# Seven block products in place of eight for gate and value in the second expert layer

## The chip, the core and the metric

The program runs on one core of one Trainium2 chip. The metric is the device time of one execution in microseconds (us). Its engines are TensorE (PE in the profile, with PEld for its weight loads), VectorE (DVE), ScalarE (ACT), GpSimd (POOL) and SyncE (SP), which issues every DMA.

## What is computed

Causal attention with a cumulative bias, then two gated expert layers, the first after a normalisation. With 2304 tokens, model width 512 and hidden width 1536 per layer, this is the part that the change touches:

```python
def _moe2_ref(x, w_gate, w_val, w_out):
    g = x @ w_gate                          # 2304x512 @ 512x1536
    silu = g * (1.0 / (1.0 + np.exp(-g)))
    val = x @ w_val                         # 2304x512 @ 512x1536
    return (silu * val @ w_out)             # 2304x1536 @ 1536x512
```

## The kernel before, in words

Every operand of a matmul is split into a high and a low part (`H`, `L`, type fp32r), and a product is three matmuls: H·H, L·H and H·L. Tokens lie in the columns: `TGROUPS` are four groups of 512 tokens and one of 256. The hidden width is cut into 12 blocks of 128 (`KF`, index `f`), the model width into 4 (`KD`).

The program has three stretches. The first holds attention and the gate and value products of the first layer. The second is the output product of the first layer: per group and `f`, the hidden block `hh` is loaded from DRAM, split on ACT (`hH`, L1050) and DVE (`hL`, L1052), and multiplied into four PSUM banks by 12 matmuls (`out_mm`, L1061); at a group's end ACT evicts the four banks (`out_store`, L1070) and the result goes to DRAM as `x1_d`. The third is the second layer: `load_x1` (L1089 to L1093) loads and splits a group of `x1`; per `f`, `gate_value` (L905) does 24 matmuls into two banks of the ring `mo`, `hidden` (L912, L914, L917) applies the gate on ACT and DVE, `split_h` splits it, and `out_mm` multiplies the block before into four other banks.

Weights come as 64-bit floats. `convert` loads a piece (L405, 512 KB) into a staging buffer (`raw` or `cvs`) and makes floats of it on ACT (`cvy`, L408) and DVE (L410), then `H` on ACT (L415) and `L` on DVE or POOL (L419). The second layer's gate and value weights (`load_gv`, 24 pieces) and output weights (`load_o`, 12 pieces) are converted during the second stretch, the last pieces through the one buffer `cvs`, and stay in SBUF.

The order of the work on each engine is fixed when the program is built: `Plan.run` gives each operation a cost and a priority (`pri`, the lower the earlier) and puts it on its engine's queue. On the chip each engine works through its queue in order and waits at each instruction for what it needs. `SLACK = 1500.0` in `Plan` keeps a matmul that another engine released back by up to 1500 ns as long as other matmuls are ready.

Of the kernel before, what the change touches and what calls it, by code (L numbers as in the profile page):

```python
# [22 lines left out]
P = 128  # L23
# [18 lines left out]
class Buf:  # L42
# [9 lines left out]
    def __call__(self):  # L52
        if self.tile is None:
            self.tile = self.make() if self.share is None else self.make(self.place)
        return self.tile

# [222 lines left out]
def tile_kernel(  # L279
# [729 lines left out]
    cvs_o = buf("o", "cvs", [P, 2 * DM], I32)  # L1009
    cvy_o = buf("o", "cvy", [P, 512], F32)  # L1010

    def load_o(src, f, pri):
        H, L = (buf("o", f"o{z}{f}", [P, DM], F32R) for z in "HL")
        if f == 0:
            plan.ops[-1]
        convert(src[f * P:(f + 1) * P, :], (H, L), 0, cvs_o, cvy_o, pri)
        return H, L

    for k in [cvs_o, cvy_o] + [buf("o", f"o{z}{f}", [1], F32) for z in "HL"
                                      for f in range(KF)] + \  # L1020
            [buf("o", f"h{z}{i}", [1], F32) for z in "hHL" for i in range(2)]:
        plan.live[k.key] = list(plan.live["o"])
    clear([cvy_o], -900)
    W1o = [load_o(w_o, f, P_ATT + 1000 + f) for f in range(KF)]
# [10 lines left out]
    def m2buf(tag, shape, dtype, name=None):  # L1035
        b = buf("m2", tag, shape, dtype, name)
        if b.key not in plan.live:
            plan.live[b.key] = list(plan.live["m2"])
        return b

    P2 = 1.0e5

    def hring(z, dtype):
        return ring("o", f"h{z}", 2, [P, 512], dtype)

    def split_h(hh, n, pri):
        H, L = hring("H", F32R), hring("L", F32R)
        op(ACT, c_act(n) + 35, lambda en: en.activation(H()[:, :n], hh()[:, :n], ACTF.Copy),  # L1050
           r=[hh], w=[H], pri=pri)
        op(DVE, c_tt(n), lambda en: en.tensor_tensor(  # L1052
            out=L()[:, :n], in0=hh()[:, :n], in1=f32(H()[:, :n]), op=ALU.subtract),
           r=[hh, H], w=[L], pri=pri, port=True)
        return H, L

    def out_mm(acc_, Wo, HL, f, n, pri):
        for d in range(KD):
            c = slice(d * P, (d + 1) * P)
            for i, (w, x) in enumerate(((0, 0), (0, 1), (1, 0))):  # L1060
                op(PE, c_mm(n), lambda en, d=d, c=c, w=w, x=x, i=i: en.matmul(  # L1061
                    acc_[d]()[:, :n], Wo[w]()[:, c], HL[x]()[:, :n], start=(f == 0 and i == 0),
                    stop=(f == KF - 1 and i == 2)), r=[(Wo[w], 0), HL[x]],
                   w=[acc_[d]] if f or d or i else [*acc_, "claim"], pri=pri)

    def out_store(acc_, n, dst, key, pri, places=("oo0", "oo1") * 2, any_engine=False):
# [111 lines left out]
```

## Time and profile before

| | before |
|---|---|
| median of 3 runs | 1134.37 us (1133.91 to 1135.48) |
| span of the profiled execution | 1134.0 us |
| PE busy | 1113.0 us (98%) |
| PEld busy | 1002.2 us (88%) |
| DVE busy | 583.3 us (51%) |
| ACT busy | 512.4 us (45%) |
| POOL busy | 181.2 us (16%) |
| DMA moved | 112.51 MB, mean 99 GB/s |

The page gives one execution, with its span as its own time; it lies 0.37 us under the median and inside the range of the runs. A matmul's duration in the records is longer than its share of the time, since matmuls overlap: the step from one start to the next is the price of one.

### The profile page before, as it was taken

What the parts mean: (1) busy time and instruction counts of PE and PEld (TensorE: products, weight loads), DVE (VectorE), ACT (ScalarE), POOL (GpSimd) and SP (SyncE); (2) the same over time, 40 slices, a digit from 0 to 9 for tenths busy, and PEclk for the clock granted to TensorE, in tenths of its full rate; (3) what the DMA queues carried; (4) which work ended last, traced back from release to release, by engine and by line L of the source; (5) the groups of instructions that cost most, each with busy time, mean ns of one, the idle gap of its engine ahead of it and who ended that gap; (6) DMA issues with size and microseconds to landing.
All of it is one profiled execution on the core that took longest, in us unless ns stands there. A gap on an engine that the chain in (4) does not pass through costs nothing.

```text
span 1134.0 us, 18700 instructions
## 1 busy us (share of the span) xinstructions
PE 1113.0 (98%) x6724; PEld 1002.2 (88%) x6724; DVE 583.3 (51%) x1606; ACT 512.4 (45%) x1135; POOL 181.2 (16%) x276
## 2 busy tenths in 40 slices
PE   8799999999999999999989999999999999999998
PEld 5599999999999999999878888888888888888898
DVE  7797778787787666547733234432222222222222
ACT  5877767667666753436744334323111211211121
POOL 3344434323333200100011000001000100100000
PEclk9999999999999999999999999999999999999999
DMA  5984443423323204359665443202000100100010
GB/s 162 291 254 117 123 133 116 124 83 110 107 85 95 62 29 147 115 160 309 203 216 175 149 126 120 89 19 75 1 1 1 65 1 1 47 1 1 1 38 19
DMA packets 70092, 112.51 MB, mean 99 GB/s; under 512 B 11568, under 2 KB 39216, under 8 KB 70000
## 3 DMA queue, kind: packets, MB, share of 16 engines
q1 hardware_dynamic: 70000, 111.33, 31.9%
q8 instruction: 53, 0.87, 0.3%
q14 instruction: 39, 0.32, 0.1%
HBM read 87.61 MB, written 23.67 MB: 98 GB/s over the span
## 4 chain that ended last, share of the span: by engine, by line
PE 48%; DMA 3%; DVE 2%; ACT 1%; issue 1%; SPq 0%; DVEq 0%; ACTq 0%
PE mo L905 26%; PE sps L1061 9%; PE tp L1061 9%; PE mo L1061 5%; DMA cvs<-in_w_gv 1%; DMA raw<-in_w_gv 1%; DMA h_d<-hh 1%; ACT H L415 1%; DVE raw L410 1%; DVE hL L1052 0%; ACT cvy L408 0%; DVE L L419 0%; DMA hh<-h_d 0%; DVE hh L917 0%; SPq L937 0%
## 5 line engine op out<-in xcount | busy, mean ns | idle before, releaser
L905 PE MATMUL mo<-xL,H 128*128 128x320 f32 (+1 forms) x768 | 228.0, 297 | 0.0
L905 PE MATMUL mo<-xH,H 128*128 128x320 f32 (+1 forms) x768 | 227.8, 297 | 0.0
L905 PE MATMUL mo<-xH,L 128*128 128x320 f32 (+1 forms) x768 | 227.7, 297 | 0.0
L914 DVE SCALAR_TENSOR_TENSOR t<-t,mo 128x256 f32<-128x256 f32 (+2 forms) x156 | 81.1, 520 | 218.3 <-ACT t L912 217.3
L905 PE MATMUL mo<-x1H,H 128*128 128x512 f32 (+1 forms) x480 | 176.6, 368 | 0.0
L905 PE MATMUL mo<-x1H,L 128*128 128x512 f32 (+1 forms) x480 | 176.6, 368 | 0.0
L905 PE MATMUL mo<-x1L,H 128*128 128x512 f32 (+1 forms) x480 | 176.6, 368 | 0.0
L912 ACT ACTIVATE t<-mo 128x256 f32<-128x256 f32 (+2 forms) x156 | 71.8, 460 | 209.5 <-PE mo L905 209.2
L1050 ACT ACTIVATE hH<-hh 128x512 fp32r<-128x512 f32 (+1 forms) x120 | 70.3, 587 | 179.8 <-DVE hh L917 126.0
L905 PEld LDWEIGHTS mo<-xH,H 128*128 128x128 f32 x768 | 144.2, 188 | 0.9 <-issue 0.2
L905 PEld LDWEIGHTS mo<-xL,H 128*128 128x128 f32 x768 | 144.3, 188 | 0.7 <-issue 0.2
L905 PEld LDWEIGHTS mo<-xH,L 128*128 128x128 f32 x768 | 144.2, 188 | 0.4
L1052 DVE TENSOR_TENSOR hL<-hh,hH 128x512 fp32r<-128x512 f32 (+1 forms) x120 | 79.6, 665 | 106.5 <-ACT hH L1050 106.1
L649 ACT ACTIVATE sc<-sc,col 128x512 f32<-128x512 f32 (+4 forms) x160 | 96.0, 600 | 65.0 <-DVE col L638 64.5
L917 DVE TENSOR_TENSOR hh<-t,mo 128x256 f32<-128x256 f32 (+2 forms) x156 | 81.1, 520 | 84.8 <-PE mo L905 81.2
L905 PEld LDWEIGHTS mo<-x1H,H 128*128 128x128 f32 x480 | 90.5, 189 | 15.0
L905 PEld LDWEIGHTS mo<-x1H,L 128*128 128x128 f32 x480 | 90.5, 189 | 14.8
L905 PEld LDWEIGHTS mo<-x1L,H 128*128 128x128 f32 x480 | 90.5, 189 | 14.8
L1093 POOL TENSOR_TENSOR x1L<-x1l,x1H 128x512 fp32r<-128x512 f32 (+1 forms) x20 | 24.4, 1226 | 417.6 <-ACT x1H L1091 392.2
L1061 PE MATMUL tp<-hH,oH 128*128 128x512 f32 (+1 forms) x192 | 69.8, 363 | 0.0
L1061 PE MATMUL tp<-hL,oH 128*128 128x512 f32 (+1 forms) x192 | 69.8, 364 | 0.0
L1061 PE MATMUL tp<-hH,oL 128*128 128x512 f32 (+1 forms) x192 | 69.6, 363 | 0.0
(133 smaller groups left out, 2017.0 us busy)
## 6 DMA issues: line engine op xcount, KB each, us to landing
raw<-in_w_gv SPq DMA_DIRECT2D x40, 511.8 KB, 6.0
hh<-h_d SPq DMA_DIRECT2D x48, 256.0 KB, 2.7
cvs<-in_w_o SPq DMA_DIRECT2D x24, 511.8 KB, 3.7
lq<-in_qk SPq DMA_DIRECT2D x32, 288.0 KB, 3.5
cb<-cum_d SPq DMA_DIRECT2D x32, 288.0 KB, 3.6
h_d<-hh SPq DMA_DIRECT2D x72, 128.0 KB, 2.5
vl<-in_vp SPq DMA_DIRECT2D x32, 160.0 KB, 2.3
x_d<-oo SPq DMA_DIRECT2D x16, 256.0 KB, 3.4
```

The source lines that it names most:

```text
L410: op(DVE, c_tt(n), lambda en: en.scalar_tensor_tensor(out=whole(U32), in0=whole(U32), scalar=13, in1=y().bitcast(U32), op0=ALU.logical_shi ...
L415: ACT: lambda en: en.activation(H()[:, cut], whole(), ACTF.Copy),
L649: op(ACT, c_act(o + m, 2) + 35, lambda en: en.activation(sc()[:m, :o + m], sc()[:m, :o + m], ACTF.Exp, scale=-1.0, bias=col()[:m, 0, t:t + 1],
L905: op(PE, c_mm(n), lambda en, a=a, x=x, c=c, k=k, i=i: en.matmul(ps()[:, :n], a()[:, c], x()[:, k, :n], start=(k == 0 and i == 0), stop=(k ...
L912: op(ACT, c_act(n), lambda en: en.activation(t()[:, :n], gp()[:, :n], ACTF.Tanh, scale=0.5), r=[gp], w=[t], pri=pri)
L914: op(DVE, c_tt(n), lambda en: en.scalar_tensor_tensor(out=t()[:, :n], in0=t()[:, :n], scalar=1.0, in1=gp()[:, :n], op0=ALU.add, op1=ALU.mu ...
L917: op(DVE, c_tt(n), lambda en: en.tensor_tensor(out=hh()[:, :n], in0=t()[:, :n], in1=vp_()[:, :n], op=ALU.mult), r=[vp_, t], w=[hh], pri=pri)
L1050: op(ACT, c_act(n) + 35, lambda en: en.activation(H()[:, :n], hh()[:, :n], ACTF.Copy), r=[hh], w=[H], pri=pri)
L1052: op(DVE, c_tt(n), lambda en: en.tensor_tensor(out=L()[:, :n], in0=hh()[:, :n], in1=f32(H()[:, :n]), op=ALU.subtract), r=[hh, H], w=[L], p ...
L1061: op(PE, c_mm(n), lambda en, d=d, c=c, w=w, x=x, i=i: en.matmul(acc_[d]()[:, :n], Wo[w]()[:, c], HL[x]()[:, :n], start=(f == 0 and i == 0) ...
L1093: op(POOL, c_ptt(n), lambda en, k=k, x=x: en.tensor_tensor(out=L()[:, k, :n], in0=x()[:, :n], in1=f32(H()[:, k, :n]), op=ALU.subtract), r= ...
```

## The change

The weights of gate and value for one `f` are seen as a 2x2 block matrix (gate and value in the rows, the two halves of the model width in the columns), and two token groups of 512 as the columns of the other factor. Strassen's scheme in Winograd's form gives the four result blocks with seven block products in place of eight. A block product is 6 matmuls of 128x512, so a pair of groups takes 42 matmuls per `f` in place of 48. Groups 0 and 1, and 2 and 3, are the pairs; group 4 (256 columns) is done as before, by `plain_unit`.

The four sums of weight blocks (`S1` to `S4`) are made per `f` in `load_w2`, and the four sums of token blocks (`T1` to `T4`) once per pair in `prepare_pair`. The loops are turned: `f` is outside, and per `f` come the first pair, group 4 and the second pair. The weights are therefore loaded and converted per `f`, through two staging buffers (`raws`, named `cvs0` and `cvs1`), into one of two places. A unit (`pair_unit`) uses three banks: bank `b` takes four products one upon the other and is copied out between them by ACT (`keep`); `c` takes two. Further sums are made on DVE (`add`) and POOL or DVE. The gated hidden blocks go to DRAM (`h2_d`), and the output product is a last stretch of its own (`out_layer`, also used for the first layer), whose weights are loaded and converted late in the last `f` and beside its first group. The output of the first layer stays in SBUF: `x1_d` and its loads are gone.

```diff
...
+    raws = [obuf(f"cvs{i}", [P, 2 * DM], I32) for i in range(2)]
...
+    def load_o(src, f, HL, pri):
+
+        H, L = HL
+        stage = raws[f % 2]
+        sub = [(POOL, c_ptt(DM)), (DVE, c_tt(DM))]
+        value = load_raw(src[f * P:(f + 1) * P, :], stage, pri)
+        op(ACT, c_act(DM) + 35, lambda en: en.activation(H(), value(), ACTF.Copy),
+           r=[stage], w=[H], pri=pri)
+        op(sub, 0, lambda en: en.tensor_tensor(out=L(), in0=value(), in1=f32(H()),
+                                               op=ALU.subtract),
+           r=[stage, H], w=[L], pri=pri, port=True)
...
+    def load_w2(f, pri):
+
+        H, L = (wide_buf(w2_tags[f % 2][z], [P, 2048], F32R, f"w2{'HL'[z]}") for z in range(2))
+        gate, val = (load_raw(w2_gv[f, :, 512 * z:512 * z + 512], raws[z], pri)
+                     for z in range(2))
...
+        for i, (a, b, sign, r) in enumerate((
+                (v1, v2, ALU.add, raws[1:]), (lambda: S(0), g1, ALU.subtract, [(sums, 0), raws[0]]),
+                (g1, v1, ALU.subtract, raws), (g2, lambda: S(1), ALU.subtract, [(sums, 1), raws[0]]))):
+            op(two, 0, lambda en, i=i, a=a, b=b, sign=sign: en.tensor_tensor(
...
+        for i, (src, r) in enumerate((
+                (gate, raws[:1]), (val, raws[1:]),
+                (lambda: sums()[:, :512], [(sums, 0), (sums, 1)]),
+                (lambda: sums()[:, 512:], [(sums, 2), (sums, 3)]))):
+            cut = slice(512 * i, 512 * i + 512)
+            op(ACT, c_act(512) + 35, lambda en, src=src, cut=cut: en.activation(
+                H()[:, cut], src(), ACTF.Copy), r=r, w=[(H, i)], pri=pri)
+            op([(POOL, c_ptt(512)), (DVE, c_tt(512))], 0, lambda en, src=src, cut=cut:
+               en.tensor_tensor(out=L()[:, cut], in0=src(), in1=f32(H()[:, cut]),
+                                op=ALU.subtract), r=[*r, (H, i)], w=[(L, i)], pri=pri, port=True)
...
+    def pair_unit(f, W, X, groups, pri):
+
+        u = units[0] % 2
+        units[0] += 1
+        b, c, d = [mo_bank() for _ in range(3)] if u == 0 else \
+            [bank(t) for t in ("sps0", "sps1", "tp0")]
+        p1, p5, u2, u3, t1, t2 = (spare_buf(6 * u + i) for i in range(6))
...
+        def product(ps, a, x, first, claims=()):
+            q = A_ROWS[a]
+            at = pri + step[0]
+            step[0] += 1
+            for kk in range(2):
+                cut = slice(q * 256 + kk * P, q * 256 + kk * P + P)
+                for i, (w, z) in enumerate(((0, "H"), (0, "L"), (1, "H"))):
+                    xx = X[x, z][kk]
+                    op(PE, c_mm(n), lambda en, w=w, xx=xx, cut=cut, kk=kk, i=i: en.matmul(
+                        ps()[:, :n], W[w]()[:, cut], xx(), start=first and kk == 0 and i == 0,
+                        stop=kk == 1 and i == 2, skip_group_check=not first), r=[(W[w], q // 2), xx],
+                       w=[ps] if kk or i else [ps, *claims], pri=at)
+
...
+        product(b, "A11", "B11", True, [c, d] if u == 0 else [])
+        keep(p1, b)
+        product(c, "S1", "T1", True)
+        keep(p5, c)
+        product(b, "S2", "T2", False)
+        keep(u2, b)
+        product(c, "S4", "B22", False)
+        add(u2, c)
+        product(b, "S3", "T3", False)
+        keep(u3, b)
+        product(d, "A12", "B21", True)
+        add(p1, d)
+        op([(POOL, c_ptt(n)), (DVE, c_tt(n))], 0, lambda en: en.tensor_tensor(
+            out=u3(), in0=u3(), in1=p5(), op=ALU.add), r=[u3, p5], w=[u3], pri=-1.0e4, port=True)
+        gated(u2, t2, u3, u3, groups[1])
+        product(b, "A22", "T4", False)
+        gated(p1, t1, b, lambda: b()[:, :n], groups[0])
...
-        a = banks(gi % 2 == 1)
-        for f in range(KF):
-            hh = hring("h", F32)
-            pri = P2 + 100 * gi + f
-            op(SP, 4 * P * n, lambda en, hh=hh, gi=gi, f=f, n=n: en.dma_start(out=hh()[:, :n],
-                                                                       in_=h_d[gi][f]),
-               r=[f"h_d{gi}"], w=[hh], pri=pri)
-            HL = split_h(hh, n, -1.0e4)
-            out_mm(a, W1o[f], HL, f, n, pri)
-            i = gi * KF + f
-            if i % 3 == 1 and i // 3 < KF:
-                W2.append(load_gv(w2_gv, i // 3, places2, lambda: cvy_o, P2 + 100 * gi + f))
-            if gi == len(TGROUPS) - 1:
-                W2o.append(load_o(w2_o, f, P2 + 100 * gi + f))
-        out_store(a, n, lambda d, gi=gi: x1_d[gi][:, d], f"x1_d{gi}", -1.0e4)
...
+        a = out_layer(gi, h_d, f"h_d{gi}", W1o, P2 + 100 * gi, gi % 2 == 1)
...
+        out_store(a, n, tiles, -1.0e4)
+        if gi == 0:
+            W2.append(load_w2(0, P2 + 100))
+        if gi == 1:
+            X2.append(pair_places(0))
+            prepare_pair(X2[0], first, x1, P2 + 150)
+        if gi == 3:
+            last = first, x1
+        if gi == 2 * NPAIR:
+            X2.append(pair_places(1))
+            prepare_pair(X2[1], *last, P2 + 350)
...
+    P3 = P2 + 1000
+    for f in range(KF):
+        if f + 1 < KF:
+            W2.append(load_w2(f + 1, P3 + 40 * f - 20))
+        pair_unit(f, W2[f], X2[0], (0, 1), P3 + 40 * f)
+        plain_unit(f, W2[f], rest, 2 * NPAIR, 256, P3 + 40 * f + 10)
+        pair_unit(f, W2[f], X2[1], (2, 3), P3 + 40 * f + 20)
...
+        load_o(w2_o, f, HL, P3 + 40 * (KF - 1) + 5 + f)
...
-        X = load_x1(gi, P2 + 1000 + 100 * gi)
-        a = banks(False)
-        HL = None
-        for f in range(KF):
-            pri = P2 + 1000 + 100 * gi + f
-            gp, vq = mo_bank(), mo_bank()
-            gate_value(gp, W2[f], X, f, 0, n, pri, [vq], ["claim"])
-            gate_value(vq, W2[f], X, f, 1, n, pri)
-            if HL is not None:
-                out_mm(a, W2o[f - 1], HL, f - 1, n, pri + 0.5)
-            t = m2buf(f"t{f % 2}", [P, 512], F32)
-            hh = hring("h", F32)
-            hidden(gp, vq, t, hh, n, -1.0e4)
-            HL = split_h(hh, n, -1.0e4)
-        out_mm(a, W2o[KF - 1], HL, KF - 1, n, P2 + 1000 + 100 * gi + KF)
...
+        a = out_layer(gi, h2_d, f"h2_d{gi}", W2o, P4 + 100 * gi, gi % 2 == 0, True)
...
```

What stands in the queues at three places (names with their buffer numbers):

In the new stretch of pair units the PE queue reads as follows for the second pair (`sps0` is bank `b`, `sps1` bank `c`; `x..T2` are parts of the token sums, `w2H` and `w2L` of the weights). The first row is the last matmul of the product with `T2`, the last row the first of that with `T3`, which goes into the same bank.

```order
L1274 MATMUL sps0_10686<-xHT2_8590,w2L_10478 128x512
L1274 MATMUL sps1_10754<-xHB22_8572,w2H_10471 128x512
L1274 MATMUL sps1_10754<-xLB22_8592,w2H_10471 128x512
...
L1274 MATMUL sps1_10754<-xHB22_8572,w2L_10478 128x512
L1274 MATMUL tp0_10765<-xHB21_8314,w2L_10478 128x512
L1274 MATMUL mo2_10789<-xHB11_7788,w2H_10655 128x512
L1274 MATMUL mo2_10789<-xLB11_7796,w2H_10655 128x512
L1274 MATMUL mo2_10789<-xHB11_7788,w2L_10662 128x512
L1274 MATMUL mo2_10789<-xHB11_7788,w2H_10655 128x512
L1274 MATMUL sps0_10686<-xHT3_8582,w2H_10471 128x512
```

Before, a bank was left alone until its product had been read for good (24 matmuls into two `mo` banks, then 12 of `out_mm`). Now 11 matmuls of other banks (6, 1 and 4) stand between two products into the same bank.

In the ACT queue at the end of the first group of the first layer's output product there stood before (`cvy`, `H9`, `H10` are conversions of second-layer weights, `oo` evictions):

```order
L415 ACTIVATE H9_7836<-raw1_7727 128x512
L1050 ACTIVATE hH1_7862<-hh1_7831 128x512
L408 ACTIVATE cvy_6349<-cvs_6351 128x512
L415 ACTIVATE H10_7881<-cvs_6351 128x512
L1050 ACTIVATE hH0_7885<-hh0_7855 128x512
L1070 ACTIVATE oo_7894<-sps0_6456 128x512
L1070 ACTIVATE oo_7900<-sps1_6466 128x512
L1050 ACTIVATE hH1_7909<-hh1_7876 128x512
L408 ACTIVATE cvy_6349<-cvs_6351 128x512
```

and now, from the change, at the same group's end (`x1` are the evictions, `xH` the splits of token blocks for the pairs):

```order
L1117 ACTIVATE hH0_7740<-hh0_7715 128x512
L1117 ACTIVATE hH1_7758<-hh1_7733 128x512
L1117 ACTIVATE hH0_7776<-hh0_7751 128x512
L1141 ACTIVATE x1_7783<-sps0_6462 128x512
L1117 ACTIVATE xHB11_7788<-x1_7783 128x512
L1141 ACTIVATE x1_7783<-sps1_6470 128x512
L1141 ACTIVATE x1_7783<-tp0_6478 128x512
L1141 ACTIVATE x1_7783<-tp1_6486 128x512
L1117 ACTIVATE hH1_7808<-hh1_7769 128x512
```

The conversions (`cvy`), each of which waits for a weight load, are gone from this place; splits of token blocks, which wait for no load, have come.

In the ACT queue where the pair units end and the last stretch begins (`u` are copies out of PSUM by `keep`, or tanh at L1289; `oH`, `o` are output weights, `cvy` their conversion, `hH` the split of hidden blocks) the change has:

```order
L1280 ACTIVATE u_10952<-sps1_10937 128x512
L1070 ACTIVATE cvy_6354<-cvs0_6356 128x512
L1280 ACTIVATE u_10968<-sps0_10862 128x512
L1051 ACTIVATE o_10973<-cvs0_6356 128x512
L1070 ACTIVATE cvy_6354<-cvs1_6371 128x512
L1289 ACTIVATE u_10991<-u_10968 128x512
L1289 ACTIVATE u_10996<-u_10939 128x512
L1051 ACTIVATE o_11002<-cvs1_6371 128x512
L1280 ACTIVATE u_11008<-sps0_10862 128x512
L1117 ACTIVATE hH0_11020<-oH11_10886 128x512
L1070 ACTIVATE cvy_6354<-cvs0_6356 128x512
L1051 ACTIVATE o_11041<-cvs0_6356 128x512
```

Copies out of bank `b` (`u_10968`, `u_11008`) now stand behind conversions that wait for a load of 512 KB.

## Rows read from the trace of the kernel before

**Rows 1.** The page: span, busy times of the engines, granted clock by slices.

```profile
span 1134.0 us, 18700 instructions
PE 1113.0 (98%) x6724; PEld 1002.2 (88%) x6724; DVE 583.3 (51%) x1606; ACT 512.4 (45%) x1135; POOL 181.2 (16%) x276
PEclk9999999999999999999999999999999999999999
```

**Rows 2.** Busy times by stretch: start:end and length, engines, granted clock, DMA share, GB/s.

```profile
565.14:603.25 38.11, 35.02 (x146) 28.17 (x145) 12.67 (x19) 16.67 (x27) 5.14 (x4) 0.96 0.63 198
603.25:635.89 32.64, 32.64 (x146) 27.04 (x145) 10.36 (x12) 12.41 (x20) 5.17 (x4) 1.00 0.50 161
635.89:668.53 32.64, 32.64 (x147) 27.04 (x146) 8.05 (x12) 9.76 (x16) 0.00 (x0) 1.00 0.44 138
797.73:895.71 97.98, 97.98 (x434) 81.04 (x433) 24.96 (x36) 19.13 (x32) 5.58 (x4) 1.00 0.06 19
```

**Rows 3.** The chain that ended last, in order of time: start, length, what.

```profile
571.81 6.33 DMA cvs<-in_w_gv
635.89 32.64 PE mo L1061 x144
797.73 5.44 PE mo L905 x24
1085.20 2.88 PE mo L905 x24
```

**Rows 4.** Who waited for whom, on PE after 440 us: total, times, longest.

```profile
PE mo L1061 <- ACT hH L1050: 3.1, 2, 2.2
```

**Rows 5.** Timeline around that wait: PE, then ACT.

```profile
570.36 0.39 PE L1061 MATMUL mo<-hH,oL 128*128 128x512 f32 x1
571.63 1.20 PE L1061 MATMUL mo<-hH,oH 128*128 128x512 f32 x4 [0.89 <-ACT hH L1050]
579.58 1.19 PE L1061 MATMUL mo<-hH,oH 128*128 128x512 f32 x4 [2.21 <-ACT hH L1050]
581.52 0.63 PE L1061 MATMUL mo<-hL,oH 128*128 128x512 f32 x1
581.95 0.63 PE L1061 MATMUL mo<-hH,oL 128*128 128x512 f32 x1
578.23 0.77 ACT L408 ACTIVATE cvy<-cvs 128x512 f16<-128x512 bf16 x1 [3.05 <-DMA cvs<-in_w_gv]
578.89 1.29 ACT L1050 ACTIVATE hH<-hh 128x512 fp32r<-128x512 f32 x2
```

**Rows 6.** Groups by line and form, 440 us on: busy, mean ns of one.

```profile
L914 DVE SCALAR_TENSOR_TENSOR t<-t,mo 128x512 f32<-128x512 f32 x48 | 33.0, 687 | 166.6 <-ACT t L912 166.5
L912 ACT ACTIVATE t<-mo 128x512 f32<-128x512 f32 x48 | 28.6, 597 | 151.4 <-PE mo L905 151.4
L1093 POOL TENSOR_TENSOR x1L<-x1l,x1H 128x512 fp32r<-128x512 f32 x16 | 21.5, 1348 | 325.6 <-ACT x1H L1091 300.2 <-DMA x_d<-oo 25.4
L408 ACT ACTIVATE cvy<-cvs 128x512 f16<-128x512 bf16 x27 | 21.3, 789 | 40.5 <-DMA cvs<-in_w_o 35.0 <-DMA cvs<-in_w_gv 5.6
L415 ACT ACTIVATE oH<-cvs 128x512 fp32r<-128x512 f32 x23 | 15.4, 668 | 11.7 <-DVE cvs L410 10.8 <-PE tp L1061 0.9
L917 DVE TENSOR_TENSOR hh<-t,mo 128x256 f32<-128x256 f32 x24 | 10.1, 420 | 11.2 <-PE mo L905 10.1 <-DMA h_d<-hh 0.8
L912 ACT ACTIVATE t<-mo 128x256 f32<-128x256 f32 x24 | 9.1, 381 | 33.2 <-PE mo L905 33.2
L1070 ACT ACTIVATE oo<-mo 128x512 f32<-128x512 f32 x8 | 4.8, 596 | 1.0 <-DMA x_d<-oo 0.5 <-PE mo L1061 0.3
```

**Rows 7.** DMA issues: count, KB each, median us from issue to landing.

```profile
cvs<-in_w_o SPq DMA_DIRECT2D x24, 511.8 KB, 3.7
cvs<-in_w_gv SPq DMA_DIRECT2D x8, 511.8 KB, 5.3
```

**Rows 8.** Timeline at the end: last matmuls, ACT, DVE.

```profile
1126.68 0.28 PE L905 MATMUL mo<-x1H,L 128*128 128x256 f32 x1
1127.00 0.42 DVE L917 TENSOR_TENSOR hh<-t,mo 128x256 f32<-128x256 f32 x1 [0.60 <-PE mo L905]
1129.56 0.28 PE L1061 MATMUL tp<-hH,oL 128*128 128x256 f32 x1
```

More of the change, by code (lines that the diff above doesn't have):

```diff
@@ L55, in __call__, with __new__, whole @@
         return self.tile
+class Part(tuple):
+    def __new__(cls, buf, part, view):
+        new = tuple.__new__(cls, (buf, part))
+        new.view = view
+        return new
+    def __call__(self):
+        return self.view(self[0]())
+def whole(x):
+    return x if isinstance(x, Part) else (x, None)
 class Plan:
@@ L1007, in tile_kernel, with later_buf @@
     op(NONE, 0, swap_at, w=at_keys + ["o"])
[L1009 to L1022, printed above, removed]
+    def later_buf(pool, tag, shape, dtype, name=None):
+        b = buf(pool, tag, shape, dtype, name)
+        if b.key not in plan.live:
+            plan.live[b.key] = list(plan.live[pool])
+        return b
@@ new lines, in out_layer @@
+        for f in range(KF):
+            hh = hring("h", F32, n)
+            op(SP, 4 * P * n, lambda en, hh=hh, f=f: en.dma_start(out=hh(), in_=h_dram[gi][f]),
+               r=[(key, f) if by_row else key], w=[hh], pri=pri + f)
+            out_mm(a, Wo[f], split_h(hh, n, -1.0e4), f, n, pri + f)
+        return a
+    NPAIR = 2
+    A_ROWS = {"A11": 0, "A12": 1, "A21": 2, "A22": 3, "S1": 4, "S2": 5, "S3": 6, "S4": 7}
+    B_ROWS = ("B11", "B21", "B22", "T1", "T2", "T3", "T4")
+    sums = m2buf("sf", [P, 1024], F32)
@@ new lines, in pair_places @@
+    def pair_places(p):
+        out = {}
+        spare = iter([f"{z}{f}" for f in range(4) for z in "HL"])
+        places = iter([f"{z}{f}" for f in range(KF) for z in "HL"][14 * p:])
+        for name in B_ROWS:
+            for z in "HL":
+                tag = next(places, None)
+                if tag is not None:
+                    b = buf("w", tag, [P, 2, 512], F32R, f"x{z}{name}")
+                    claim(b)
+                    out[name, z] = [Part(b, kk, lambda t, kk=kk: t[:, kk, :]) for kk in range(2)]
+                else:
+                    out[name, z] = [Part(obuf("o" + next(spare), [P, 512], F32R, f"x{z}{name}"),
+                                         None, lambda t: t[:, :]) for _ in range(2)]
+        return out
@@ new lines, in plain_unit @@
+    def plain_unit(f, W, X, gi, n, pri):
+        gp, vq = mo_bank(), mo_bank()
+        wH, wL = W
+        xH, xL = X
+        for z, ps in ((0, gp), (1, vq)):
+            for k in range(KD):
+                q = 2 * z + k // 2
+                c = slice(256 * q + P * (k % 2), 256 * q + P * (k % 2) + P)
+                for i, (a, x) in enumerate(((wH, xH), (wH, xL), (wL, xH))):
+                    op(PE, c_mm(n), lambda en, a=a, x=x, c=c, k=k, i=i, ps=ps: en.matmul(
+                        ps()[:, :n], a()[:, c], x[k](), start=(k == 0 and i == 0),
+                        stop=(k == KD - 1 and i == 2)), r=[(a, q // 2), x[k]],
+                       w=[ps] if k or i or z else [ps, vq], pri=pri)
+        t, hh = (m2buf(f"tmp{i}", [P, 512], F32, ("t", "hh")[i]) for i in range(2))
+        hidden(gp, vq, t, hh, n, -1.0e4)
+        op(SP, 4 * P * n, lambda en: en.dma_start(out=h2_d[gi][f], in_=hh()[:, :n]),
+           r=[hh], w=[(f"h2_d{gi}", f)], pri=-1.0e4)
```

203 lines of the change are left out of this document (165 added, 38 removed).

## The prediction

> **What bounds the kernel now.** I read the page first: PE is busy for 1113.0 of 1134.0 us, every slice of its clock shows the top digit, and no other engine is above 51% [rows 1]. A busy PE need not be PE at its peak, so next I read the busy times by stretch, from the point where the first layer's output product is alone on PE. A group of 512 tokens there takes 32.64 us, twice running, with PE busy throughout and a granted clock of 1.00 (the 2.4 GHz level); the second layer takes 97.98 us for a group of 432 matmuls, which is 0.2268 us each [rows 2]. The chain that ended last says the same in its own way: from 579.58 us on it is PE alone, and 144 matmuls of 512 columns stand in it as one piece of 32.64 us [rows 3]. So one matmul of 128x512 costs 32.64 / 144 = 0.2267 us, one of 256 columns 2.88 / 24 = 0.120 us [rows 3], and in this half of the program time is the number of matmuls times these steps.
>
> One stretch is off this pace: the second group of the first layer's output product took 38.11 us and not 32.64, at a mean clock of 0.96 [rows 2]. After 440 us PE waited there alone, twice, 3.1 us in all, for ACT's `hH` [rows 4]. The timeline tells why: ACT stood at a conversion (`cvy`) for 3.05 us, since a weight load into `cvs` landed late, and the `hH` that PE needed was behind it in the queue [rows 5]. That load took 6.33 us [rows 3]; the median of its kind is 5.3, and that of the output weights 3.7 [rows 7]. After the second wait the step between matmuls was 0.43 us (581.52 to 581.95) [rows 5], the 1.2 GHz level, for eight matmuls: 8 x 0.2 = 1.6 us of the loss.
>
> **The change, part by part.**
>
> *Matmuls removed.* Two pairs times 12 values of `f` are 24 units, each with 42 matmuls where 48 stood: 144 matmuls of 128x512 less; no other matmul is added or resized. At 0.2267 us that is 32.64 us, all of it on the path, since PE does nothing else in this half [rows 2, 3]. The Trainium skill, "TensorE: Matmul & The Clock Gate", section "Back-to-back issue gap", gives about 131 ns for a matmul of 512 columns in a stream with weight loads. By that the saving would be 18.9 us; this trace disagrees, its step is 226.7 ns.
>
> *The late conversion.* Before, 24 pieces of second-layer weights were converted within the first layer's output product. Now only two values of `f` are, both before the first group ends, and at that group's end ACT has evictions and splits that wait for no load. Stores and reloads of `x1` are gone too, so the DMAs that crowded the late load are fewer. I take the whole 38.11 - 32.64 = 5.47 us back [rows 2]. Bounds: 0 if another late load takes its place, 5.47 if nothing does; the value is nearest to the group after it, which ran at pace [rows 2].
>
> *The wait that is added: one bank for four products.* Three times per unit `b`, and once `c`, must be read before PE may go on in it. The chain: the record of a 512-column matmul is 0.39 us for a step of 0.227 [rows 5], so it ends 0.16 after its step; the reader starts 0.04 later (1126.68 + 0.28 to 1127.00) [rows 8]; the copy takes 0.596 [rows 6]; PE starts some 0.05 after the end of an ACT instruction (578.89 + 0.64 to 579.58) [rows 5]. Sum 0.85 us. In the queue at least 11 matmuls of other banks stand in between: 11 x 0.2267 = 2.49 us. The cover is 1.64 us, so I cost this at nothing; with the cover gone it is 0.85 us, 24 x 4 = 96 times.
>
> *Do the other engines keep up?* One `f` lasts 84 x 0.2267 + 24 x 0.120 = 21.9 us. ACT has 8 copies at 0.596, 4 tanh at 0.597 and one at 0.381, two `cvy` at 0.789 and four splits at 0.668 [rows 6]: 11.8 us, 54%. DVE has 18 instructions of 512 columns at about 0.69 and four of 256 at 0.420 [rows 6]: 14.1 us, 64%. POOL has two splits at 1.35 and two sums of 256, for which no row stands; at twice the 512-column price they would still leave it idle for most of `f`. DMAs: 1 MB of weights and 1.1 MB of hidden blocks per 21.9 us, about 100 GB/s, below the 138 to 161 GB/s beside which groups ran at pace [rows 2]. So these are hidden. So are the token sums: a pair's take 24 instructions of about 0.69 us, 16.6 us of DVE with POOL's help. The first pair's have a group of 32.64 us, in which DVE was busy for 8 to 10 us [rows 2]; the second pair's have the last group, 144 x 0.120 = 17.3 us, and 9.5 us of the first unit.
>
> *The hand-over to the last stretch.* Twelve output-weight loads are squeezed into the last `f` and the first group after it, among stores and loads of hidden blocks. There the copies of bank `b` for the products `T3` and `T4` stand behind conversions. Lower bound nothing: at the 3.7 us of a quiet load [rows 7] no one waits. Upper bound 5.47 us, a repeat of the place that has such a crowd in this trace [rows 2]. A load as late as the worst (6.33, against 3.7: 2.6 us) eats the cover of 1.64 us and leaves a wait of 1.0 us, the same as the first of the two old waits (570.36 + 0.23 to 571.63 is 1.04), after which the step did not change [rows 5]. I take 1.0 us, once.
>
> *The end.* The last matmul starts at 1129.56 us [rows 8] and the evictions and stores after it are as before: nothing.
>
> The sum against the profiled execution: 1134.0 - 32.6 - 5.5 + 1.0 = 1096.9 us. That span is 0.4 us under the median of the runs, so I forecast 1097.3 us. A measurement of this kernel can tell about 0.2%, 2.3 us, from no change.
>
> **The rivals.**
>
> *A crowd at the hand-over, 0.22.* The old wait comes back where the output weights are loaded: once 5.47 us in place of 1.0, 1101.8 us; at both borders of the pair stretch 10.9, 1107.2 us. For it: ACT's queue there has the same pattern as where it went wrong before, and the weights come in at the same time as the hidden blocks. Against it: the groups at 138 and 161 GB/s converted output weights as well and lost nothing [rows 2].
>
> *A late load in every `f`, 0.12.* In the pair stretch the two `cvy` of the next but one `f` stand in ACT's queue ahead of the copies of the second pair. If their loads are as late as the worst one, each of ten `f` loses 1.0 us: 1096.3 + 10 = 1106.3 us. Against it: these loads meet only the five stores of an `f`, where the late one met stores and reloads of `x1` and of `hh`.
>
> *The old wait stays, 0.05.* The conversions that remain in the first layer's output product, or the preparation of sums on ACT, hold up an `hH` as before: 1102.8 us.
>
> *Slower, 0.04: every bank change is exposed.* ACT and DVE hand a bank back later than the order of the queue assumes, in every unit. The gain of 38.1 us is used up at 38.1 / 96 = 0.40 us per re-use, that is, when the chain of 0.85 us takes 2.9 us and more, with queueing of 2 us before each copy; fully uncovered, without any order in between, it is 96 x 0.85 = 81.6 us, 1178 us. For it: PSUM copies that were once per product are now in the middle of one. Against it: 54% of ACT and eleven matmuls of cover. The Trainium skill speaks for this rival: "Perfetto Trace Analysis", section "Matmuls", asks that independent groups rotate through different banks, so that the eviction of one overlaps the matmuls of the next. Here products return to the same bank; the queue puts the other pair's banks between them, and no row of before shows whether that is enough.
>
> **How the numbers follow.** The forecast has 0.57. Its own range is 1095.0 to about 1099: without a new wait it is 1096.3, less 0.46 for the spread of the runs below their median and 0.8 for the rounding of the steps. The range of 1095.0 to 1109.0 adds the crowd at both borders and the late load in every `f`; outside are the slower case and the tails of the others. Faster by over 0.2%: all cases but the last and a sliver, 0.95; within 0.2%: 0.01, since that needs the waits to meet the gain by chance; slower: 0.04.
>
> **What would show it.** In the profile after, PE must have 144 instructions less, and a stretch of one `f` in the pair stretch should last 21.9 us with PE and clock at full; the second group of the first output product should be one piece of 32.6 us in the chain; waits of PE for ACT should be few and lie at the end of the pair stretch, behind a `cvy` that waits for `in_w2_o`. The forecast is wrong if one `f` takes more than 22.5 us (then look for who waits for `keep`, or for a `cvy` behind `in_w2_gv`), if the granted clock falls in the pair stretch, or if a wait for `hH` is found again after the first group.

## The result, and the profile after

The changed kernel takes 1098.34 us (median of four runs, 1097.29 to 1102.02), the kernel before 1134.14 us on the same chip: a ratio of 0.9689, 95% interval 0.9670 to 0.9708. The forecast was 1097.3 us, faster with 0.95.

The page of the changed kernel, to be laid beside [rows 1]: span, busy times, granted clock by slices.

```profile
span 1096.1 us, 19019 instructions
PE 1078.8 (98%) x6580; PEld 973.5 (89%) x6580; DVE 675.9 (62%) x1755; ACT 583.5 (53%) x1266; POOL 208.1 (19%) x300
PEclk9999999999999999999999999999999999999999
```

PE has 144 instructions fewer (6724 to 6580) and is busy for 34.2 us less; DVE and ACT have 92.6 and 71.1 us more to do, and still neither is above 62%. PE bounds the kernel as before.

The same kernel, busy times by stretch, with the columns of [rows 2]: the second group of the first output product, two blocks (values of `f`) of the pair stretch, and a group of the last stage.

```profile
564.74:597.49 32.75, 32.75 (x145) 26.95 (x144) 11.89 (x18) 12.21 (x22) 0.00 (x0) 1.00 0.34 97
755.19:777.15 21.96, 21.96 (x111) 18.64 (x110) 14.74 (x23) 11.05 (x20) 4.48 (x4) 1.00 0.28 104
777.15:799.11 21.96, 21.96 (x111) 18.64 (x110) 14.74 (x23) 11.03 (x20) 4.47 (x4) 1.00 0.33 114
1010.01:1042.65 32.64, 32.64 (x146) 27.03 (x145) 8.32 (x12) 9.87 (x16) 0.00 (x0) 1.00 0.42 129
```

The group that took 38.11 us takes 32.75, at 97 GB/s where it was 198 [rows 2], and nothing is left on POOL there. A block takes 21.96 us (forecast 21.9), with DVE at 14.74 (14.1) and ACT at 11.05 us (11.8). PE is busy without a gap in all four.

What PE waited for after 430 us, in the view of [rows 4]:

```profile
PE mo L921 <- DVE x L905: 0.8, 1, 0.8
PE tp L1132 <- DVE hL L1120: 0.3, 1, 0.3
```

The two waits for ACT's `hH` are gone; neither of these two lies in the pair stretch. In the chain that ended last, the second group of the first output product is now one piece:

```profile
564.91 32.75 PE mo L1132 x144
```

### The profile page after: what moved, and what is told of

It reads as the page before. It is cut to its first block, busy times and chain, and to the rows that moved or that the text cites. A ratio compares the mean times of both kernels' runs of the same rounds, so it can differ in the third digit from the quotient of the medians.

```text
span 1096.1 us, 19019 instructions
## 1 busy us (share of the span) xinstructions
PE 1078.8 (98%) x6580; PEld 973.5 (89%) x6580; DVE 675.9 (62%) x1755; ACT 583.5 (53%) x1266; POOL 208.1 (19%) x300
## 4 chain that ended last, share of the span: by engine, by line
PE 84%; DMA 3%; DVE 2%; ACT 1%; issue 1%; POOLq 0%; POOL 0%; ACTq 0%; DVEq 0%; SPq 0%
PE mo L921 23%; PE mo L1132 12%; PE mo L1274 10%; PE sps L1274 8%; PE tp L1132 6%; PE sps L1132 6%; PE tp L708 4%; PE tp L692 4%; PE sps L628 4%; PE mo L1325 3%; DMA cvs<-in_w_o 2%; PE tp L1274 1%; PE mo L828 1%; ACT cvy L1070 1%; DVE cvs L1074 0%
## 5 line engine op out<-in xcount | busy, mean ns | idle before, releaser
L930 DVE SCALAR_TENSOR_TENSOR t<-t,mo 128x256 f32<-128x256 f32 (+1 forms) x108 | 48.1, 445 | 40.4 <-ACT t L928 39.4
L692 PE MATMUL tp<-ident,sc 128*128 128x128 f32 x432 | 65.5, 276 | 0.0
L700 DVE TENSOR_TENSOR pTB<-tp,pTB 128x512 fp32r<-128x512 f32 (+1 forms) x96 | 54.4, 575 | 14.5 <-ACT pTB L697 12.4
L933 DVE TENSOR_TENSOR hh<-t,mo 128x256 f32<-128x256 f32 (+1 forms) x108 | 48.0, 445 | 18.9 <-PE mo L921 18.0
L1132 PE MATMUL mo<-hL,oH 128*128 128x512 f32 (+1 forms) x144 | 54.4, 378 | 0.0
L628 PE MATMUL sps<-kHH,qst 128*128 128x288 f32 (+4 forms) x160 | 54.2, 346 | 0.0
L1132 PE MATMUL mo<-hH,oH 128*128 128x512 f32 (+1 forms) x144 | 54.0, 377 | 0.0
L1132 PE MATMUL mo<-hH,oL 128*128 128x512 f32 (+1 forms) x144 | 53.8, 377 | 0.0
L1289 ACT ACTIVATE u<-u 128x512 f32<-128x512 f32 x48 | 29.7, 633 | 43.7 <-DVE u L1284 43.7
L654 DVE CUSTOM_DVE_ANT_0 sc<-sps,cb 128x384 f32<-128x384 f32 (+3 forms) x112 | 48.9, 443 | 6.4 <-PE sps L628 5.3
L697 ACT ACTIVATE pTB<-tp 128x512 fp32r<-128x512 f32 (+1 forms) x96 | 47.0, 502 | 10.9 <-PE tp L692 5.9
```

The source lines that it names most:

```text
L628: op(PE, c_mm(n), lambda en, pt=pt, o=o, c=c, n=n, z=z, kk=kk: en.matmul(pt()[:, :n], qst[j]()[:, o:o + 128], kk()[:, c:c + n], start=z == ...
L654: op(DVE, c_tt(w), lambda en: en.tensor_tensor_reduce(out=sc()[:m, c:c + w], in0=pt()[:m, c - at:c - at + w], in1=bias()[:m, c + off:c + o ...
L692: op(PE, C_TR, lambda en, pt=pt, a=a, m=m, kb=kb, t=t: en.transpose(pt()[:, a:a + P], self.sc[t]()[:, kb * P:kb * P + P], ident()), r=[sel ...
L700: op(DVE, c_tt(n), lambda en, pt=pt, a=a, d0=d0, n=n, kn=kn: en.tensor_tensor(out=L()[:kn, d0:d0 + n], in0=pt()[:kn, a:a + n], in1=f32(H() ...
L930: op(DVE, c_tt(n), lambda en: en.scalar_tensor_tensor(out=t()[:, :n], in0=t()[:, :n], scalar=1.0, in1=gp()[:, :n], op0=ALU.add, op1=ALU.mu ...
L933: op(DVE, c_tt(n), lambda en: en.tensor_tensor(out=hh()[:, :n], in0=t()[:, :n], in1=vp_()[:, :n], op=ALU.mult), r=[vp_, t], w=[hh], pri=pri)
```

## The experiments

Each kernel is compared with the kernel before, run on the same chip (medians of 1133.3 to 1134.2 us). My theory was that the gain is 144 matmuls at 0.2267 us plus the 5.5 us of the old stall, with the re-use of the banks hidden.

**Eight products again.** In the pair unit:

```diff
         product(d, "A12", "B21", True)
+        product(d, "A12", "B21", False)
         add(p1, d)
```

> The changed kernel with the product A12*B21 made twice in each of the 24 pair units, so that a unit has eight products again and everything else of the change stays (the second copy is added to the first, so the output is not the reference's). My theory: the gain is the 144 matmuls of 128x512 that the change saves at 0.2267 us each, plus what the late weight conversion cost. Then this kernel is 144 x 0.2267 = 32.6 us slower than the changed one, about 1131 us (1129.5 to 1132.5), and stays about 3 us ahead of the kernel before. Rival: the new arrangement (separate output stage, the interleaved units) gives part of the gain itself, by filling gaps that the old one had: then the step is smaller than 32.6 us, the kernel is at 1120 to 1128 us.

Measured: 1130.63 us (1129.02 to 1132.74), ratio to before 0.9969, interval 0.9957 to 0.9982. That is 32.3 and 32.5 us above the changed kernel (1098.34 us, and 1098.17 in the repeat below, on another chip), and by the ratios to the kernel before 31.8 and 32.1 us, against 32.64 from the count. Its block, by stretch:

```profile
763.22:787.90 24.68, 24.68 (x122) 20.90 (x120) 13.47 (x22) 10.95 (x20) 5.38 (x5) 1.00 0.26 91
```

24.68 - 21.96 = 2.72 us for 12 matmuls, 0.2267 us each. So in the pair stretch the arrangement itself gives nothing, and the matmuls give what their step says. The rest of the gain, 1134.22 - 1130.63 = 3.6 us (2.0 to 4.9 by the interval), stands where the forecast had 5.5 - 1.0 = 4.5. The Trainium skill, "TensorE: Matmul & The Clock Gate", section "Back-to-back issue gap", gives about 131 ns for 512 columns in a stream with weight loads; by an estimate from it, 144 x 0.131, this kernel would have been 18.9 us slower than the changed one. The run disagrees: 32 us are some 222 ns per matmul, and the block shows 226.7.

**Order of the products.** In the planner, the preference for work just released taken away from the pair stretch on (the condition holds for the last stage too):

```diff
-                    slack = self.SLACK
+                    slack = self.SLACK if ops[n][3] < 1.01e5 else 0.0
```

> The changed kernel with the planner's preference for work that another engine has just released switched off in the pair stretch, so that products of the two pairs stand in another order there. My theory: the accumulator banks are given back with time to spare in nearly any order of the products (0.85 us of chain against at least 1.36 us for the six matmuls of another product), so the time stays within 2 us of the changed kernel, 1097 to 1101 us. Rival: only this order hides the re-use of the banks; then it is 5 to 20 us slower, 1103 to 1118 us.

Measured: 1101.9 us (1100.65 to 1103.22), ratio 0.9721, interval 0.9705 to 0.9737: just above my bound and below the rival's. The blocks are as long as in the changed kernel:

```profile
755.19:777.15 21.96, 21.96 (x109) 18.66 (x108) 14.56 (x23) 11.03 (x20) 3.29 (x3) 1.00 0.30 107
```

In its profile PE waited twice for a bank, 1.1 us in all. Its first matmul of the pair stretch started at 667.79 us, 3.6 us after that of the changed kernel (664.22; in its second profile, below, 666.00), though all that stands ahead is the same: in these profiles most of the difference lies ahead of the edit.

**One unit after another.** All matmuls of the pair stretch chained in the order of the code, so that only a unit's own products stand between two uses of a bank:

```diff
-                       w=[ps] if kk or i else [ps, *claims], pri=at)
+                       w=[ps, "serial"] if kk or i else [ps, "serial", *claims], pri=at)
```

(and the same in `plain_unit`.)

> The changed kernel with the matmuls of the pair stretch chained in the order in which they are written, unit after unit, so that no other unit's matmuls stand between two products; within a unit a bank is still used again only behind a product of six matmuls in another bank. My theory: the cover is then 6 x 0.2267 = 1.36 us against a chain of some 0.85 to 1.0 us, still enough: 1097.5 to 1101 us. Rival: it is the interleaving with the other pair that hides the re-use; with 96 re-uses and 0.1 to 0.4 us showing at each it is 10 to 38 us slower, 1108 to 1136 us.

Measured: 1100.5 us (1096.95 to 1102.53), ratio 0.9705, interval 0.9681 to 0.9730, so no slower than can be told from the changed kernel. Its block, by stretch:

```profile
728.50:750.46 21.96, 21.96 (x110) 18.68 (x109) 14.59 (x24) 11.03 (x20) 3.30 (x3) 1.00 0.30 102
```

And the only waits of PE for a bank, in the view of who waited for whom:

```profile
PE mo L1274 <- ACT u L1280: 0.6, 2, 0.4
```

Six matmuls of another bank are cover enough: of 96 re-uses two showed, 0.6 us. The interleaving with the other pair isn't what hides them.

**A bank used again at once.** As the last kernel, and `A12*B21` moved ahead, so that `T4` follows `T3` into the same bank, once in each of 24 units:

```diff
+        product(d, "A12", "B21", True)
+        add(p1, d)
         product(b, "S3", "T3", False)
         keep(u3, b)
-        product(d, "A12", "B21", True)
-        add(p1, d)
```

> As the kernel with its units chained, and the product A12*B21 moved ahead of S3*T3, so that the last product of each unit goes into the bank that the matmul just before wrote and that ScalarE has yet to copy out: one uncovered re-use in each of 24 units. My theory: each shows the whole chain, from the usual next start of a matmul to the end of the copy (about 0.2 us to the last matmul's end, 0.60 us of copy, 0.2 us back to TensorE): 24 x 0.85 to 1.05 us, 20 to 25 us slower than the chained kernel, about 1119 to 1124 us. Rival: the re-use of a bank costs little even uncovered (the copy keeps ahead of the new writes): within 5 us of the chained kernel.

Measured: 1134.54 us (1128.71 to 1139.05), ratio 1.0006, interval 0.9989 to 1.0023: 34 us slower than the chained kernel, the whole gain gone. Both theories missed; mine had the mechanism and too small a price. PE's timeline at two of the places, then ACT's:

```profile
779.08 0.39 PE L1274 MATMUL sps<-xHT,w2L 128*128 128x512 f32 x1
780.74 0.50 PE L1274 MATMUL sps<-xHT,w2H 128*128 128x512 f32 x1 [1.27 <-ACT u L1280]
...
790.40 0.39 PE L1274 MATMUL mo<-xHT,w2L 128*128 128x512 f32 x1
791.61 0.50 PE L1274 MATMUL mo<-xHT,w2H 128*128 128x512 f32 x1 [0.82 <-ACT u L1280]
791.94 0.39 PE L1274 MATMUL mo<-xLT,w2H 128*128 128x512 f32 x1
```

```profile
779.58 0.63 ACT L1289 ACTIVATE u<-u 128x512 f32<-128x512 f32 x1 [1.36 <-DVE u L1284]
780.11 0.58 ACT L1280 ACTIVATE u<-sps 128x512 f32<-128x512 f32 x1
```

From one start to the next it is 1.21 us at 791.61 and 1.66 at 780.74, so 0.98 and 1.43 us over the step. In the second case ACT was at a `tanh` (L1289) when the bank was full, and the copy began 0.64 us after the record of the product's last matmul ended (779.08 + 0.39 = 779.47). Over all 24 places the mean is 1.33 us (0.57 to 2.5), and the matmul after it takes a step of 0.33 and not 0.23 us (791.61 to 791.94): 1.44 us in all, 24 times 34.5 us. The profile is of the longest of the ten executions (1139.05 us), so it fits the median less closely than these figures suggest. The Trainium skill, "Perfetto Trace Analysis", section "Matmuls", asks that independent groups rotate through banks, so that copying one out overlaps the matmuls of the next. The traces agree and show how little is enough here: another bank's six matmuls in between.

**The old stall: conversions placed later.** In the kernel before, the planner is told that the loads of the last two weight blocks land later:

```diff
-            done = 2300.0 + took - ns
+            done = 2300.0 + took - ns + lands
...
-                    early)
+                    early, 4000 if src is w2_gv and f + 2 >= KF else 0)
```

> The kernel before, with one thing changed: the planner is told that the four raw halves of the last two gate and value weight blocks, which pass through the one staging buffer, land 4 us later than it had assumed, so that it places their conversions (and the split of the hidden activations) in another order on ScalarE and VectorE. All eight products stay. My theory: of the 36 us gained by the change 5.5 us came from the stall in the second group of the first output product, which was the conversion standing ahead of the split on ScalarE while its transfer was late; taken away alone it gives about 1128.7 us (1127.5 to 1130), ratio 0.995, and that group takes 32.7 us in place of 38.1. Rival: the stall is made of transfers that collide and only moves to another place; then 1132.5 to 1135 us.

Measured: 1132.09 us (1129.04 to 1136.06), ratio 0.9984, interval 0.9972 to 0.9995: 1.7 us gained and not 5.5. In the profile the split no longer stands behind a late conversion. What stands there now is the eviction of the first group, which waits for its tile, that is, for a store of the first layer's output:

```profile
567.30 1.24 ACT L1070 ACTIVATE oo<-tp 128x512 f32<-128x512 f32 x2 [3.25 <-DMA x_d<-oo]
568.57 1.27 ACT L1050 ACTIVATE hH<-hh 128x512 fp32r<-128x512 f32 x2
```

**The kernel before once more, and the changed one.**

> The kernel before once more, for another profile. My theory: the first stretch (all that stands ahead of the first output product) differs from the first profile by up to 2 us, as it does between the two profiles at hand, while the second group of the first output product again takes about 38 us with the same two waits on ScalarE's split. Rival: the stall in that group is a chance of the one profiled execution; then the group takes 32.7 us here.

Measured: one execution, 1131.95 us, span 1129.8. The waits are there again:

```profile
574.83 0.77 ACT L408 ACTIVATE cvy<-cvs 128x512 f16<-128x512 bf16 x1 [2.31 <-DMA cvs<-in_w_gv]
575.48 1.27 ACT L1050 ACTIVATE hH<-hh 128x512 fp32r<-128x512 f32 x2
```

The group took 36.45 us (562.12 to 598.57), with the clock at 1.00 throughout, where the first profile had 37.95 between the same matmuls. And the first matmul of the first output product's long run stood at 532.46 us in place of 535.70: 3.24 us of difference in a stretch that is the same code in the same order.

> The changed kernel once more, for another profile and more times. My theory: the fixed stretches of the second expert layer take the same to 0.1 us (32.6 us for a group of the output product, 21.96 us for a block of the pair stretch) and what varies by 2 to 4 us between executions is the first stretch, ahead of the change. Rival: the variation of 1097 to 1102 us comes from the new stages, from waits at the hand-over that come and go.

Measured: 1098.17 us (1097.33 to 1100.72), ratio 0.9686, interval 0.9671 to 0.9701. The group took 32.64 us, a block 21.96 again; so those hold. But there was a wait at the hand-over to the last stage that the first profile had not: ACT's timeline,

```profile
957.58 0.79 ACT L1070 ACTIVATE cvy<-cvs 128x512 f16<-128x512 bf16 x1 [3.21 <-DMA cvs<-in_w_o]
959.13 0.66 ACT L1051 ACTIVATE o<-cvs 128x512 fp32r<-128x512 f32 x1 [0.76 <-DVE cvs L1074]
959.69 0.61 ACT L1117 ACTIVATE hH<-hh 128x512 fp32r<-128x512 f32 x1
```

and PE's:

```profile
960.36 0.73 PE L1132 MATMUL mo<-hH,o 128*128 128x512 f32 x2 [1.22 <-ACT hH L1117]
```

**Output weights left out.** Eight of twelve loads and conversions at the hand-over taken away:

```diff
+        if f >= 4:
+            W2o.append(W2o[f % 4])
+            continue
         W2o.append(HL)
```

> The changed kernel without the loads and conversions of eight of the twelve blocks of the second layer's output weights, all of which fall at the hand-over to the last stage; those products use the first four blocks again, so the output is not the reference's. My theory: the hand-over costs nothing that shows, since the products that still run cover the loads; the time stays within 1 us of the changed kernel. Rival (my own forecast's term, and the crowded hand-over): the late load costs 1.0 us, or 4 to 9 us when crowded, in most executions; then this kernel is faster by that.

Measured: 1097.82 us (1096.01 to 1098.18), ratio 0.9674, interval 0.9661 to 0.9688: 0.4 us under the changed kernel on the same chip, and the intervals overlap. Its profile has no wait for ACT at the hand-over. So the late load costs 0 to 1.2 us there, by execution; a crowd of 4 us and more showed in no profile.

**Four tiles for the first layer's output.** The kernel before, with two tiles that lie idle in that stage (`t0`, `t1`) added to the two that carry the output to DRAM, once with the conversions placed later and once without:

```diff
-        out_store(a, n, lambda d, gi=gi: x1_d[gi][:, d], f"x1_d{gi}", -1.0e4)
+        out_store(a, n, lambda d, gi=gi: x1_d[gi][:, d], f"x1_d{gi}", -1.0e4,
+                  ("oo0", "oo1", "t0", "t1"))
```

> The kernel before with the conversions placed as for transfers that land 4 us later, and in addition four tiles in place of two for the first layer's output on its way to DRAM, so that ScalarE's copy of the third bank no longer waits for the store of the first. All eight products stay. My theory, mended after the last runs: the 4.1 to 5.6 us that the first output product lost in the two profiles of the kernel before have two causes on ScalarE's queue, the late weight load and, hidden behind it, the wait of the copies for the stores; with both gone the stretch of the first output product loses under 0.5 us, and the time is 4 to 5 us below the kernel before, 1128.5 to 1130.5 us. Rival: the 2.0 us that were left with the conversions placed later are a matter of busy transfers (loads of weights, reloads of the stored activations) and stay: then 1131 to 1133 us.

> The kernel before with only the four tiles for the first layer's output, the conversions where they were. My theory: the late weight load still stands ahead of the split on ScalarE, as its wait ends last there, so 3 to 5 us of loss stay in that stretch and the time is within 1.5 us of the kernel before. Rival: the stores were the cause all along, and the load only looked late beside them: then as fast as the kernel with both, 1128.5 to 1130.5 us.

Measured: 1142.91 us, ratio 1.0088 (1.0074 to 1.0102), and 1140.32 us, ratio 1.0064 (1.0049 to 1.0079). Both slower than the kernel before, which no theory had. Part of it is a wait of my own making: the second layer needs `t0` and `t1`, and at its start PE waited 4.6 and 4.4 us and went on with ten steps of 0.43 us (701.72 to 705.95 in the kernel with the tiles alone). With the tiles alone the group itself lost 2.2 us (34.83 - 32.64), less than in the kernel before, and what else made that kernel slower is not accounted for. With both edits the old stall came back in another form. SyncE's queue in that kernel:

```profile
563.63 2.25 SPq L1075 DMA_DIRECT2D x_d<-oo  x4
565.99 1.62 SPq L1105 DMA_DIRECT2D hh<-h_d  x2
567.66 0.94 SPq L1089 DMA_DIRECT2D x1l<-x_d  x2
```

And ACT's timeline:

```profile
571.60 0.63 ACT L1050 ACTIVATE hH<-hh 128x512 fp32r<-128x512 f32 x1 [6.01 <-DMA hh<-h_d]
```

The four stores now go out together, the activations `hh` are issued behind them, and ACT waits 6.01 us for those. PE then waited 2.87 us, and the group took 38.77 us. The late transfer is a different one each time. The Trainium skill, "DMA: Bandwidth & Descriptors", section "Queues, rings and completion order", says that each DMA engine takes the descriptors of a ring in order. The trace fits that: these two activations, behind four stores on one queue, landed 5.1 to 5.5 us after their issue, where the median of their kind is 2.7; the order of descriptors itself no run here shows.

**Loads taken away, and loads put back.** In the kernel before, the loads that were late are left out:

```diff
-                W2.append(load_gv(w2_gv, i // 3, places2, lambda: cvy_o, P2 + 100 * gi + f))
+                W2.append(load_gv(w2_gv, i // 3, places2, lambda: cvy_o, P2 + 100 * gi + f)
+                          if i // 3 + 2 < KF else W2[i // 3 - 2])
```

> The kernel before without the loads and conversions of the last two of the twelve gate and value blocks, the only ones of that layer that pass through the one staging buffer while the first output product runs; their products use the blocks ten and eleven places earlier in the list again (blocks 8 and 9), so the output is not the reference's. All eight products, the stores of the first layer's output and their reloads stay. My forecast's reading (the late load alone made the stall): the stretch of the first output product loses under 0.5 us and the time is 4 to 5.5 us below the kernel before, 1128 to 1130 us. Rival, after the runs with conversions placed later and with four tiles: the load is one of several kinds of transfer on SyncE's one queue (loads of weights, stores of the layer's output, reloads of it), and with it gone the copies still wait for the stores; then 1.5 to 2.5 us of loss stay and the time is 1130.5 to 1132.5 us.

Measured: 1131.83 us (1130.1 to 1136.39), ratio 0.9986, interval 0.9973 to 0.9998: 1.7 us gained, as the rival had it. ACT again waits for a store, and then for `hh`:

```profile
568.35 0.60 ACT L1070 ACTIVATE oo<-tp 128x512 f32<-128x512 f32 x1 [3.10 <-DMA x_d<-oo]
...
575.67 1.30 ACT L1050 ACTIVATE hH<-hh 128x512 fp32r<-128x512 f32 x2 [0.73 <-DMA hh<-h_d]
```

And in the changed kernel, in the second group of its first output product, four of the loads put back, with the first part of their conversions (no split into `H` and `L`):

```diff
+            if gi == 1 and key[:3] == "h_d" and f % 3 == 0:
+                load_raw(w2_gv[10 + f // 6, :, 512 * (f // 3 % 2):512 * (f // 3 % 2) + 512],
+                         raws[0], pri + f, [HL[0]])
```

> The changed kernel with four loads and half-conversions of gate and value weights, whose results nobody uses, put back into the second group of its first output product, through one staging buffer, as the kernel before has them there. Nothing else is put back: no stores of the layer's output to DRAM, no reloads. My forecast's reading (a load that lands late behind the planner's back is enough): the wait of TensorE on the split returns, 2 to 5 us slower than the changed kernel, 1100 to 1103.5 us. Rival: the load is late only because stores and reloads share the queue with it; with 14 loads of activations alone beside it it lands in time, and the time stays within 1 us of the changed kernel, 1097 to 1099.5 us.

Measured: 1098.52 us (1093.97 to 1099.56), ratio 0.9676, interval 0.9652 to 0.9699: no slower. Its group, by stretch:

```profile
565.28:597.99 32.71, 32.71 (x145) 26.95 (x144) 14.56 (x22) 15.12 (x27) 0.00 (x0) 1.00 0.53 161
```

And one of the added conversions on ACT, which waits for its load as the old ones did, but for 0.79 us:

```profile
575.13 0.79 ACT L1070 ACTIVATE cvy<-cvs 128x512 f16<-128x512 bf16 x1 [0.79 <-DMA cvs<-in_w_gv]
```

So the loads with `hh` alone beside them make no stall. The second group of the first output product, between the same matmuls in all profiles:

| kernel | us | GB/s | transfers that it shares the queue with |
|---|---|---|---|
| before; again | 37.95; 36.45 | 197; 204 | weights, stores, reloads, `hh` |
| before, conversions later | 34.39 | 198 | the same |
| before, late loads left out | 34.37 | 158 | stores, reloads, `hh` |
| before, four tiles; and conversions later | 34.83; 38.77 | 214; 178 | weights, stores, reloads, `hh` |
| changed; again | 32.75; 32.64 | 97; 96 | `hh` |
| changed, loads put back | 32.71 | 161 | weights, `hh` |

Mean bandwidth doesn't decide: 158 GB/s lost 1.7 us, 161 GB/s nothing. In this group each kernel with stores and reloads on the queue loses 1.7 us or more, with or without the late loads; those without them lose 0.1 us at most, also with the loads. But stores and reloads on the queue are not enough for a loss. The third group has the same four stores and the reloads at its start, and it kept its pace; first the kernel with the late loads left out, second group and third, then the third group of the kernel with the conversions later, which has a load of weights besides:

```profile
564.42:598.79 34.37, 33.32 (x146) 26.80 (x144) 8.74 (x13) 12.40 (x21) 5.16 (x4) 1.00 0.51 158
598.79:631.48 32.69, 32.69 (x145) 27.02 (x144) 10.45 (x12) 12.40 (x20) 5.17 (x4) 1.00 0.52 161
597.55:630.19 32.64, 32.64 (x146) 27.04 (x144) 9.56 (x14) 13.34 (x22) 5.16 (x4) 1.00 0.59 182
```

Of the six profiles of kernels with stores and reloads, five have a third group of 32.64 to 32.80 us; in the sixth (four tiles and conversions later) it took 34.82. What makes the second group different stays open. Open too is whether it is the transfers on the queue or the instructions on ACT that wait for them (evictions for a store, splits of `x1` for a reload): the changed kernel has neither. Store and reload were not tried apart.

## Why the prediction was right, and where it was not

- **Matmuls removed, -32.64 us: right.** Putting the eighth product back costs 32 us, and 2.72 us a block.
- **Late conversion, -5.47 us: right in sign, too narrow in cause, and too large by 0.2 us in one profile of before and 1.7 in the other.** The step read the stall as a late load ahead of `hH` [rows 5] and took its whole price back. The change does take the whole stall away, but the load's leaving is not enough to explain it: in the kernel before, without the load, 1.7 us came back, and in the changed kernel, with the loads put back, nothing was lost. In these runs the stall went away in full only with the stores and reloads of `x1`, and with the instructions on ACT that wait for them; the forecast named these transfers only in passing. They are not the whole cause either, since the group after kept its pace with them, and the rest is open. The stall's size was read from one execution: 5.3 us (37.95 - 32.64) there and 3.8 us in the second profile, which had waits nearly as long (2.7 against 3.1 us in all) but no fallen clock.
- **Bank re-use, 0 us: right.** It was too cautious about the cover (six matmuls do) and too cheap about the price: 0.85 us was forecast for an uncovered one, and 1.44 measured, since ACT is often at something else when the bank is full and the matmul after the wait is slow. The slower rival's full price of 81.6 us would by this have been 96 x 1.44 = 138 us; its condition never came about.
- **Other engines keep up: right,** with 21.96 us a block in every profile and no wait in it; the rival of a late load in every `f` had no case.
- **Hand-over, +1.0 us: right in place, and in form but for the victim.** The sum priced a copy of bank `b` behind the conversions; what waited was an `hH` behind a `cvy` that waits for output weights, 0 in one profile and 1.2 us in another. No crowd came.
- **The base, +0.4 us: too small by about 1.5 us.** I took the span of the profiled execution as its time, here and in the table of the time before. Runs lie 1.75 to 2.15 us above their spans (1097.84 against 1096.1, 1131.95 against 1129.8), so that execution took about 1135.9 us and was one of the longer ones, with a first stretch that varies by 3 us. Less 32.6 and 5.3, and with 0 to 1.2 for the hand-over, it gives 1098.0 to 1099.2 us, and 1098.3 was measured. That the forecast came within 1.0 us is in part luck: a base too low and a hand-over that the first profile doesn't show went against each other.
- **The end, nothing: right within 0.6 us.** From the last matmul's start to the end of the span it is 3.8 us (1092.28 to 1096.1) where it was 4.4 [rows 1, 8].

## What to carry to other kernels

Where a stretch runs at the pace of its matmuls, count them and multiply by the step that the trace shows. Before crediting a change with an old stall, ask whose turn comes when the late transfer is gone: here, with loads, stores and reloads on one queue, another transfer stood in its place each time, and only the kernel without stores and reloads lost nothing. Look, too, for a stretch that has the suspected cause and no loss, as the third group had. An accumulator bank could take several products in turn here with six matmuls of another bank between; without them each turn cost 1.44 us.

## What was not expected of the hardware

- After a wait the first matmul of 512 columns took a step of 0.33 us (791.61 to 791.94) in place of 0.2267, even where the next steps were at full pace.
- The clock fell to its 1.2 GHz level (steps of 0.43 us) after some waits and not after others: in the kernel with the bank used at once after a gap of 1.84 us in the records, for some 3 us (817.85 to 821.05; the steps of 256 columns there are 0.21 us in place of 0.12), in the kernel before after 2.21 us, but not in its second profile after 1.95 us.
- Two executions of the kernel before came to the same matmul of the first output product 3.24 us apart (532.46 and 535.70 us), though the code ahead of it and its order are the same; differences of 2 us between kernels are therefore not read from one profile each.
